# Rezero sum of two streams: three 64 KiB slots with the scaled operand multiplied in place, instead of two wide and two narrow buffers with a fused multiply-add

## The chip, the cores and the metric

The kernel runs on one core of a Trainium2 chip. The metric is device time in microseconds (us). The kernel before took 151.99 us, the median of three runs from 151.8 to 152.13. A profile is one execution recorded by the hardware profiler; its times count from the first instruction of the program.

## The reference

```python
B, S, D = 512, 32, 640
x     : (512, 32, 640) bf16
fx    : (512, 32, 640) bf16
alpha : (1,) bf16

def reference(x, fx, alpha):
    return x + alpha * fx
```

Each of x, fx and the result is 20.97 MB. Every element of x and fx is read once, every element of the result is written once, and there is one multiplication and one addition for each.

## The kernel before, in words

The three arrays are seen as 128 rows, one for each partition of the on-chip memory, of 81,920 elements (160 KiB) each. A unit K is 1,024 elements (2 KiB). The work is cut along the row, and differently for x and fx: x and the result in pieces of 32, 32 and 16 units (64, 64 and 32 KiB a partition), fx in pieces of 16, 16, 19, 16 and 13 units (32, 32, 38, 32 and 26 KiB). Two buffers of 64 KiB a partition hold pieces of x (`x_t`), two of 38 KiB hold pieces of fx (`f_t`). A third piece of x therefore needs the first buffer back, which is free once the first store has landed; a third piece of fx needs a VectorE pass to be over.

VectorE works on each overlap of a piece of fx with a piece of x, in one instruction, `scalar_tensor_tensor` (L92): it multiplies fx by alpha and adds x, and writes the sum over x. There are six of these. Alpha comes as a single value; a matrix product with a row of ones (L115) spreads it over the 128 partitions and VectorE copies it from PSUM to the fp32 tile `a_f` (L117).

Every transfer is issued by SyncE, whose queue works in program order: an issue that has to wait holds up all later ones. The order is written out by hand in `PLAN`, where `x i` and `f j` are loads (L77 and L85), `c j i` is a pass on VectorE, `s i` is a store (L104), and `a` fetches alpha (L111 and after). The first piece of x is cut into three transfers, of 8, 28 and 28 KiB a partition:

```python
X = [(0, 32), (32, 64), (64, 80)]
FX = [(0, 16), (16, 32), (32, 51), (51, 67), (67, 80)]
X_CUTS = {0: (4, 18)}
# order: x0  a  f0 f1 x1  c00  f2  c10  s0  f3 x2  c21  f4  c31 c32  s1  c42  s2
```

A load of 38 KiB a partition moves 4,864 KB in one transfer, spread over 16 DMA engines, eight partitions to each; a packet is the row of one partition.

At the end a no-op on SyncE waits for everything but the last store, which the exit itself waits for.

Of the kernel before, what the change touches and what calls it, by code (L numbers as in the profile page):

```python
# [2 lines left out]

# [4 lines left out]

ACT = mybir.ActivationFunctionType
ALU = mybir.AluOpType  # L10
F32 = mybir.dt.float32
BF16 = mybir.dt.bfloat16

K = 1024
P = 128


X = [(0, 32), (32, 64), (64, 80)]
FX = [(0, 16), (16, 32), (32, 51), (51, 67), (67, 80)]

X_CUTS = {0: (4, 18)}
PLAN = """
x 0
a
f 0
f 1
x 1
c 0 0
f 2
c 1 0  # L30
s 0
f 3
x 2
c 2 1
f 4
c 3 1
c 3 2
s 1
c 4 2
s 2  # L40
"""


@with_exitstack
def kernel(
    ctx: ExitStack,
    tc: tile.TileContext,
    x: bass.AP,
    fx: bass.AP,
    alpha: bass.AP,  # L50
    out: bass.AP,
):

    nc = tc.nc
    xv = x.flatten_outer_dims().rearrange("(p n) d -> p (n d)", p=P)
    fxv = fx.flatten_outer_dims().rearrange("(p n) d -> p (n d)", p=P)  # L60
    ov = out.flatten_outer_dims().rearrange("(p n) d -> p (n d)", p=P)
    assert xv.shape[1] == X[-1][1] * K == FX[-1][1] * K

    consts = ctx.enter_context(tc.tile_pool(name="consts", bufs=1))
    psum = ctx.enter_context(tc.tile_pool(name="psum", bufs=1, space=bass.MemoryType.PSUM))
    wide = ctx.enter_context(tc.tile_pool(name="wide", bufs=2))
    fs = ctx.enter_context(tc.tile_pool(name="fs", bufs=2))
    ctx.enter_context(tc.manual_schedule())

    xt, ft = {}, {}  # L70
    done = []

    def load_x(i):
        a, b = X[i]
        xt[i] = wide.tile([P, max(e - s for s, e in X) * K], x.dtype, tag="x", name="x_t")
        for c, d in pairwise((a, *X_CUTS.get(i, ()), b)):
            r = nc.sync.dma_start(  # L77
                out=xt[i][:, (c - a) * K : (d - a) * K], in_=xv[:, c * K : d * K]
            )
            done.append(r)  # L80

    def load_f(j):
        a, b = FX[j]
        ft[j] = fs.tile([P, max(e - s for s, e in FX) * K], fx.dtype, tag="f", name="f_t")
        r = nc.sync.dma_start(out=ft[j][:, : (b - a) * K], in_=fxv[:, a * K : b * K])  # L85
        done.append(r)

    def compute(j, i):
        (fa, fb), (xa, xb) = FX[j], X[i]
        a, b = max(fa, xa), min(fb, xb)  # L90
        piece = xt[i][:, (a - xa) * K : (b - xa) * K]
        r = nc.vector.scalar_tensor_tensor(  # L92
            out=piece,
            in0=ft[j][:, (a - fa) * K : (b - fa) * K],
            scalar=lanes["a_f"][:],
            in1=piece,
            op0=ALU.mult,
            op1=ALU.add,
        )
        done.append(r)  # L100

    def store(i):
        a, b = X[i]
        r = nc.sync.dma_start(out=ov[:, a * K : b * K], in_=xt[i][:, : (b - a) * K])  # L104
        done.append(r)

    lanes = {}

    def alpha_to_lanes():
        a_1 = consts.tile([1, 1], alpha.dtype, name="a_1")  # L110
        done.append(nc.sync.dma_start(out=a_1[:], in_=alpha[None, :]))  # L111
        ones = consts.tile([1, P], alpha.dtype, name="ones")
        nc.vector.memset(ones[:], 1.0)  # L113
        a_ps = psum.tile([P, 1], F32, name="a_ps")
        done.append(nc.tensor.matmul(a_ps[:], ones[:], a_1[:], start=True, stop=True))  # L115
        lanes["a_f"] = consts.tile([P, 1], F32, name="a_f")
        nc.vector.tensor_copy(out=lanes["a_f"][:], in_=a_ps[:])  # L117

    does = {"x": load_x, "f": load_f, "c": compute, "s": store, "a": alpha_to_lanes}
    for step in PLAN.split("\n"):  # L120
        if step:
            what, *of = step.split()
            does[what](*map(int, of))


    rest = nc.sync.nop(nofuse=True)
    info = mybir.DependencyInfo(mybir.DependencyClass.Sync, mybir.DependencyReason.DATA)
    for i in done[:-1]:
        tc.add_manual_dep(rest.ins, i.ins.name, info, reason="all but the last store")


# [1 line left out]
_INS = ['x', 'fx', 'alpha']  # L133
_OUTS = [((512, 32, 640), 'bfloat16')]


# [23 lines left out]
```

## Time and profile before

| | |
|---|---|
| median of three runs | 151.99 us (151.8 to 152.13) |
| profiled execution, first to last instruction | 150.6 us; its own time outside the span is not recorded |
| bytes read / written | 41.94 MB / 20.97 MB |
| mean rate over the span | 418 GB/s |
| share of the DMA engines' time, queue q1 | 97.9% |
| VectorE busy | 86.8 us (58%) |
| PE and POOL busy | 0.2 us each |
| large transfers issued by SyncE | 13, and the one of alpha |

A row of a group gives line, engine, operation, output and inputs, shape, count, busy time and the mean of one in ns, and then the idle time of the engine before it with what ended it. A row of the timeline gives start and duration in us. "SPq" is SyncE's queue: its rows are issues, whose duration is the time to hand the transfer over and not the time to move it. In a row of the windows the last two numbers are the share of the DMA engines' time and the rate in GB/s; packets are counted in the window in which they begin. "Landing" is the moment at which a transfer's semaphore is complete.

### The profile page before, as it was taken

The page shows a single profiled execution, that of the slowest core. Times are in us where ns is not written, and L with a number is a line of the kernel's source. Part 1 is how long each engine was busy: PE and PEld are TensorE (multiplying, and loading weights), DVE is VectorE, ACT ScalarE, POOL GpSimd, SP SyncE. Part 2 cuts the span into 40 slices and gives each one's busy share as a digit, 9 for nine tenths or more (in the row PEclk, how much of TensorE's full clock was granted, in tenths as well). Part 3 has the DMA queues.
Part 4 walks back from the last instruction along what each step waited for, and adds up shares of the span by engine and source line. Part 5 has one row for each costly group of instructions (what it writes and reads, how often), then busy time and mean ns, then how long its engine had stood idle before and what let it go on. Part 6 is the DMA issues. An engine that isn't in the chain of part 4 may idle for free.

```text
span 150.6 us, 81 instructions
## 1 busy us (share of the span) xinstructions
PE 0.2 (0%) x1; PEld 0.1 (0%) x1; DVE 86.8 (58%) x8; POOL 0.2 (0%) x4
## 2 busy tenths in 40 slices
PE   0000000000000000000000000000000000000000
PEld 0000000000000000000000000000000000000000
DVE  0000000049999999970299999105999999980000
POOL 0000000000000000000000000000000000000000
DMA  5998999999969696999796997999999969698993
GB/s 183 461 472 381 480 390 418 444 479 444 583 278 557 278 557 278 496 455 341 309 557 296 539 487 313 444 426 418 418 434 410 618 278 557 296 539 374 426 435 157
DMA packets 1874, 62.92 MB, mean 418 GB/s; under 512 B 210, under 2 KB 210, under 8 KB 210
## 3 DMA queue, kind: packets, MB, share of 16 engines
q1 hardware_dynamic: 1874, 62.92, 97.9%
HBM read 41.94 MB, written 20.97 MB: 418 GB/s over the span
## 4 chain that ended last, share of the span: by engine, by line
DMA 53%; DVE 34%; SPq 1%; issue 0%; DVEq 0%
DMA f_t<-in_fx_dram 53%; DVE x_t L92 34%; SPq L77 1%; SPq L111 0%; DVEq L92 0%
## 5 line engine op out<-in xcount | busy, mean ns | idle before, releaser
L92 DVE SCALAR_TENSOR_TENSOR x_t<-f_t,a_f,x_t 128x16384 bf16<-128x16384 bf16 (+3 forms) x6 | 86.5, 14438 | 25.8 <-DMA f_t<-in_fx_dram 25.8
L117 DVE COPY a_f<-a_ps 128x1 f32<-128x1 f32 x1 | 0.2, 159 | 21.6 <-PE a_ps L115 21.6
L113 DVE MEMSET ones<- 1x128 bf16 x1 | 0.2, 165 | 0.8 <-PEq L144 0.8
L115 PE MATMUL a_ps<-a,ones 1*128 1x1 bf16 x1 | 0.2, 158 | 22.4 <-DMA a<-in_alpha_dram 22.4
L144 POOL MEMSET const-bfloat16-1.0<- 128x1 bf16 x1 | 0.1, 102 | 0.0
L144 POOL MEMSET const-uint8-127<- 128x1 uint8 x1 | 0.1, 102 | 0.0
L115 PEld LDWEIGHTS <-ones 1*128 1x128 bf16 x1 | 0.1, 100 | 1.0 <-DVE ones L113 1.0
L144 POOL MEMSET const-float32-1.0<- 128x1 f32 x1 | 0.1, 99 | 0.0
L144 POOL MEMSET const-float32-0.0<- 128x1 f32 x1 | 0.1, 98 | 0.2 <-issue 0.2
## 6 DMA issues: line engine op xcount, KB each, us to landing
f_t<-in_fx_dram SPq DMA_DIRECT2D x3, 4096.0 KB, 36.1
x_t<-in_x_dram SPq DMA_DIRECT2D x2, 3584.0 KB, 16.8
f_t<-in_fx_dram SPq DMA_DIRECT2D x1, 4864.0 KB, 24.6
x_t<-in_x_dram SPq DMA_DIRECT2D x1, 4096.0 KB, 19.3
out_dram<-x_t SPq DMA_DIRECT2D x1, 4096.0 KB, 14.9
f_t<-in_fx_dram SPq DMA_DIRECT2D x1, 3328.0 KB
x_t<-in_x_dram SPq DMA_DIRECT2D x1, 1024.0 KB, 4.7
out_dram<-x_t SPq DMA_DIRECT2D x2, 24.9
```

What stands on the lines that cost most here:

```text
L77: r = nc.sync.dma_start(out=xt[i][:, (c - a) * K : (d - a) * K], in_=xv[:, c * K : d * K])
L92: r = nc.vector.scalar_tensor_tensor(out=piece, in0=ft[j][:, (a - fa) * K : (b - fa) * K], scalar=lanes["a_f"][:], in1=piece, op0=ALU.mult ...
L113: nc.vector.memset(ones[:], 1.0)
L115: done.append(nc.tensor.matmul(a_ps[:], ones[:], a_1[:], start=True, stop=True))
L117: nc.vector.tensor_copy(out=lanes["a_f"][:], in_=a_ps[:])
L144: nc = _bacc.Bacc("TRN2", target_bir_lowering=False, num_devices=1)
```

## The change

Both inputs are now cut alike, in pieces of 64, 64 and 32 KiB a partition (a unit K is now 512 elements, 1 KiB). There are three slots of 64 KiB a partition, a, b and c. The first piece of fx goes to slot a, in transfers of 8 and 56 KiB; alpha follows; the first piece of x goes to b, the second of fx to c. VectorE multiplies a piece of fx by alpha in place (`tensor_scalar`), and adds it into the piece of x (`tensor_tensor`), six instructions in all. The second piece of x goes over the first piece of fx, in slot a, once that was added; the third pieces of fx and x share slot b, once the first store has landed. The order on SyncE is: fx0 (two transfers), alpha, x0, fx1, store 0, x1, fx2, x2, store 1, store 2. VectorE's is: multiply fx0, add x0, multiply fx1, add x1, multiply fx2, add x2. Fetching and spreading alpha is as before, as is the no-op at the end.

```diff
-K = 1024
+K = 512
...
-X = [(0, 32), (32, 64), (64, 80)]
-FX = [(0, 16), (16, 32), (32, 51), (51, 67), (67, 80)]
-
-X_CUTS = {0: (4, 18)}
...
+WIDE = 64
+PIECES = [(0, 64), (64, 128), (128, 160)]
+HEAD = 8
...
-    wide = ctx.enter_context(tc.tile_pool(name="wide", bufs=2))
-    fs = ctx.enter_context(tc.tile_pool(name="fs", bufs=2))
+    slots = ctx.enter_context(tc.tile_pool(name="slots", bufs=1))
...
+    slot = [slots.tile([P, WIDE * K], x.dtype, name=f"slot_{n}") for n in "abc"]
...
+    def move(out, in_):
+        r = nc.sync.dma_start(out=out, in_=in_)
+        done.append(r)
+        return r
...
+    def load(of, piece, at, cut=0):
...
+        a, b = piece
+        n, where = at
+        t = slot[n][:, where * K : (where + b - a) * K]
+        if cut:
+            move(t[:, : cut * K], of[:, a * K : (a + cut) * K])
+        move(t[:, cut * K :], of[:, (a + cut) * K : b * K])
+        return t
...
-        r = nc.vector.scalar_tensor_tensor(
-            out=piece,
-            in0=ft[j][:, (a - fa) * K : (b - fa) * K],
-            scalar=lanes["a_f"][:],
-            in1=piece,
-            op0=ALU.mult,
-            op1=ALU.add,
-        )
...
+    def scaled(f):
+        done.append(nc.vector.tensor_scalar(out=f, in0=f, scalar1=a_f[:], scalar2=None, op0=ALU.mult))
...
+    def added(xt, f):
+        done.append(nc.vector.tensor_tensor(out=xt, in0=xt, in1=f, op=ALU.add))
...
+    def store(piece, t):
+        a, b = piece
+        move(ov[:, a * K : b * K], t)
...
+    p0, p1, p2 = PIECES
+    f0 = load(fxv, p0, (0, 0), cut=HEAD)
...
+    x0 = load(xv, p0, (1, 0))
+    scaled(f0)
+    f1 = load(fxv, p1, (2, 0))
+    added(x0, f0)
+    scaled(f1)
+    store(p0, x0)
+    x1 = load(xv, p1, (0, 0))
+    added(x1, f1)
+    f2 = load(fxv, p2, (1, 0))
+    x2 = load(xv, p2, (1, WIDE // 2))
+    scaled(f2)
+    store(p1, x1)
+    added(x2, f2)
+    store(p2, x2)
```

More of the change, by code (lines that the diff above doesn't have):

```diff
@@ L1 @@
 from contextlib import ExitStack
-from itertools import pairwise
 import concourse.bass as bass
@@ L7 @@
 from concourse._compat import with_exitstack
-ACT = mybir.ActivationFunctionType
 ALU = mybir.AluOpType
 F32 = mybir.dt.float32
-BF16 = mybir.dt.bfloat16
-K = 1024
+K = 512
 P = 128
-X = [(0, 32), (32, 64), (64, 80)]
-FX = [(0, 16), (16, 32), (32, 51), (51, 67), (67, 80)]
-X_CUTS = {0: (4, 18)}
[L22 to L41, printed above, removed]
+WIDE = 64
+PIECES = [(0, 64), (64, 128), (128, 160)]
+HEAD = 8
 @with_exitstack
@@ L61 @@
     ov = out.flatten_outer_dims().rearrange("(p n) d -> p (n d)", p=P)
-    assert xv.shape[1] == X[-1][1] * K == FX[-1][1] * K
+    assert xv.shape[1] == PIECES[-1][1] * K
     consts = ctx.enter_context(tc.tile_pool(name="consts", bufs=1))
     psum = ctx.enter_context(tc.tile_pool(name="psum", bufs=1, space=bass.MemoryType.PSUM))
-    wide = ctx.enter_context(tc.tile_pool(name="wide", bufs=2))
-    fs = ctx.enter_context(tc.tile_pool(name="fs", bufs=2))
+    slots = ctx.enter_context(tc.tile_pool(name="slots", bufs=1))
@@ L68 @@
     ctx.enter_context(tc.manual_schedule())
-    xt, ft = {}, {}
+    slot = [slots.tile([P, WIDE * K], x.dtype, name=f"slot_{n}") for n in "abc"]
     done = []
[L73 to L78, printed above, removed]
-            )
-            done.append(r)
@@ L82, in load_f @@
[L82 to L85, printed above, removed]
-        done.append(r)
[L88 to L92, printed above, removed]
-            out=piece,
-            in0=ft[j][:, (a - fa) * K : (b - fa) * K],
-            scalar=lanes["a_f"][:],
-            in1=piece,
-            op0=ALU.mult,
-            op1=ALU.add,
-        )
-        done.append(r)
@@ L102, in store @@
[L102 to L123, printed above, removed]
+    def move(out, in_):
+        r = nc.sync.dma_start(out=out, in_=in_)
+        done.append(r)
+        return r
[7 more added lines that the diff above has]
+        return t
@@ new lines, in scaled @@
+    def scaled(f):
[7 more added lines that the diff above has]
+    f0 = load(fxv, p0, (0, 0), cut=HEAD)
+    a_1 = consts.tile([1, 1], alpha.dtype, name="a_1")
+    move(a_1[:], alpha[None, :])
+    ones = consts.tile([1, P], alpha.dtype, name="ones")
@@ new lines @@
+    nc.vector.memset(ones[:], 1.0)
+    a_ps = psum.tile([P, 1], F32, name="a_ps")
+    done.append(nc.tensor.matmul(a_ps[:], ones[:], a_1[:], start=True, stop=True))
+    a_f = consts.tile([P, 1], F32, name="a_f")
+    nc.vector.tensor_copy(out=a_f[:], in_=a_ps[:])
+    x0 = load(xv, p0, (1, 0))
[8 more added lines that the diff above has]
+    x2 = load(xv, p2, (1, WIDE // 2))
```

## The prediction

> **What bounds the kernel now.** I read the page first, then busy time by windows cut where a transfer begins, then the timeline of SyncE's queue, then groups by form. The page says how little is left to gain:
>
> ```profile
> span 150.6 us, 81 instructions
> ...
> PE 0.2 (0%) x1; PEld 0.1 (0%) x1; DVE 86.8 (58%) x8; POOL 0.2 (0%) x4
> ...
> q1 hardware_dynamic: 1874, 62.92, 97.9%
> HBM read 41.94 MB, written 20.97 MB: 418 GB/s over the span
> ```
>
> All transfers go through one queue, and its packets fill 97.9% of the 16 engines' time. The chain of waits names f_t loads and VectorE, but VectorE waits for transfers that never stop: the bound is the stream of 62.92 MB, and only holes in it are worth money. The windows show where they are (time, length, busy time of PE, PEld, DVE, POOL, clock, DMA share, GB/s):
>
> ```profile
> 0.00:1.73 1.73, 0.00 (x0) 0.10 (x1) 0.17 (x1) 0.20 (x4) 1.00 0.00 0
> 1.73:4.57 2.84, 0.00 (x0) 0.00 (x0) 0.00 (x0) 0.00 (x0) 1.00 1.00 363
> ...
> 21.53:40.99 19.46, 0.16 (x1) 0.00 (x0) 8.90 (x2) 0.00 (x0) 1.00 1.00 431
> 40.99:60.32 19.33, 0.00 (x0) 0.00 (x0) 19.33 (x2) 0.00 (x0) 1.00 1.00 434
> 60.32:68.94 8.62, 0.00 (x0) 0.00 (x0) 6.41 (x1) 0.00 (x0) 1.00 1.01 433
> 68.94:73.14 4.20, 0.00 (x0) 0.00 (x0) 0.00 (x0) 0.00 (x0) 1.00 1.01 296
> 73.14:92.46 19.32, 0.00 (x0) 0.00 (x0) 18.21 (x1) 0.00 (x0) 1.00 1.00 434
> 92.46:119.70 27.24, 0.00 (x0) 0.00 (x0) 18.69 (x3) 0.00 (x0) 1.00 1.00 433
> 119.70:139.02 19.32, 0.00 (x0) 0.00 (x0) 15.09 (x2) 0.00 (x0) 1.00 1.00 434
> ```
>
> Nothing moves until 1.73; the first MB comes at 363 GB/s, 2.84 us where 434 would need 2.42, so a pipe that starts empty loses 0.42. After that loads and stores alike run at 431 to 434, but for one stretch just ahead of the first store: 4.20 us at 296 move 1.24 MB, which 433 would move in 2.87. I call it the slow stretch; it costs 1.3 us and nothing in the profile names its cause.
>
> ```profile
> 0.73 1.33 SPq L77 DMA_DIRECT2D x_t<-in_x_dram  x3
> ...
> 49.56 0.33 SPq L85 DMA_DIRECT2D f_t<-in_fx_dram  x1
> 66.76 0.35 SPq L104 DMA_DIRECT2D out_dram<-x_t  x1
> 67.16 0.49 SPq L85 DMA_DIRECT2D f_t<-in_fx_dram  x1
> ...
> 117.40 17.96 SPq L104 DMA_DIRECT2D out_dram<-x_t  x2
> ```
>
> Every issue after the first comes well ahead of its turn: the first store is issued at 66.76 and moves from 73.14, the second at 117.40 and moves from 119.70. That lead keeps the queue full. The only start on an empty queue is 0.73 to 1.73: 1.00 us from issue to first packet. The price of a VectorE pass:
>
> ```profile
> L92 DVE SCALAR_TENSOR_TENSOR x_t<-f_t,a_f,x_t 128x16384 bf16<-128x16384 bf16 x2 | 34.5, 17282 | 9.5 <-DMA f_t<-in_fx_dram 9.5
> L92 DVE SCALAR_TENSOR_TENSOR x_t<-f_t,a_f,x_t 128x13312 bf16<-128x13312 bf16 x2 | 28.2, 14085 | 8.8 <-DMA f_t<-in_fx_dram 8.8
> ```
>
> The difference, 3.197 us for 3,072 elements, is 1.04 ns each, and 0.2 us are fixed. A fused pass over 32,768 elements would take 2 x 17.07 + 0.2 = 34.3 us.
>
> **The change part by part.** *The bytes* are the same, so the stream at full rate is too. *Longer rows, fewer transfers:* the packets of an engine fall from 104 to 80 (eight a transfer: thirteen large transfers become ten). Two loads in 32 KiB rows took 19.46 us, one in 64 KiB rows 19.33: 0.13 for eight packets, though part of it may be noise, as 90 KiB in rows of 32, 32 and 26 KiB took 27.24 against 27.18 at the price of 64 KiB rows. For 24 packets that bounds the gain between 0.1 and 0.4; I take 0.2, nearer to the longer and cleaner row.
>
> *The start:* the first issue is 8 KiB a partition as before, so 1.73 and the ramp stay. Alpha stood behind 64 KiB of x and now stands behind 64 KiB of fx; it is in the lanes at 22.7 as before (PE waited 22.4 us for it). The five transfers to f1 need no wait. 128 KiB a partition have moved at 41.0, and the one that ends there (second f_t load before, x0 after) lands at about 41.9: issued at 2.9, the largest f_t landing is 39.0 us. 192 KiB have moved at 60.3.
>
> *VectorE:* each fused pass becomes a multiply and an add. No row prices either. From above, each takes a fused pass's 1.04 ns an element, 34.3 us; from below, only the fixed 0.2 us. I take half the fused price each, an estimate: the fused pass does both operations, and if its price is theirs added, the two halves together cost what it did: 17.2 + 0.1, so 17.3 us on 32,768 elements, and 8.7 on 16,384. The multiplies have room at that price: f0's runs from 22.7 to 40.0, below x0's landing at 41.9 (it may take 19.2); f1's lies under store and load of the next 39 us; f2's ends at 126.
>
> The Trainium skill, VectorE: DVE Perf Modes, section "The perf-mode tier table (the rule you actually need)", says that bf16 adds of two tensors in SBUF run at twice, and one-tensor multiplies at four times, the basic rate. Beside the row's 1.04 ns that makes 17.1 and 8.5 us before fixed cost, as estimates by that page; no row here shows either form. By the unhalved row the time would be the 214 us of rival three; by the page it is my forecast.
>
> *First hand-over:* the add of x0 runs from 41.9 to 59.2. Behind it on SP wait the store p0 and, behind that, the load x1, which needs the same add (it overwrites f0's slot). SP issues 0.03 us after VectorE ends (66.73 to 66.76), so at 59.25; the first packet is ready 1.00 later, at 60.25, and f1's packets end at 60.32. The lead of 2.3 to 6.4 us before shrinks to the bare 1.0. From below it costs nothing; from above the empty pipe's 0.42 and the whole 1.0, together 1.4. I take 0.3, nearer to 0.42 as both ends coincide within 0.1.
>
> The Trainium skill, DMA: Bandwidth & Descriptors, section "Latency and other measured facts", gives about 0.6 us to a first byte; the trace differs, with 1.00. By that page the store would be ready at 59.85, both hand-overs would cost nothing, and the time would be 151.8.
>
> *Middle:* store p0 moves until 79.9, x1 until 99.3. SP stands at f2, whose half of slot b needs store p0 landed (0.5 after its end, 80.5); x2, store p1 and p2 queue behind it. That wait is covered: x1 has 19 us left. f2 ends at 108.9, x2 at 118.6. *Second hand-over:* x1 lands at 100.2, its add ends at 117.5, the store is issued at 117.55 and ready at 118.55, against x2's end at 118.6: again 0.3. *End:* multiply f2 to 126.2, add x2 to 134.9, its store issued 3 us before store p1 ends at 138.2. The tail is as before: 32 KiB rows, landing, exit.
>
> *Slow stretch:* kept, 1.3 us, at zero change; bounds 0 and -1.3.
>
> Sum: 150.6 + 0.3 + 0.3 - 0.2 = span 151.0. What lies around the profiled span is shown only through the runs (151.8 to 152.13), whose median is 1.4 above it; so 152.4.
>
> **The rivals.** *One, faster: the slow stretch goes.* If it comes with a store that queues early behind a load (6.4 us ahead at 66.76), the late stores don't have it. For it: at 117.40 a store came 2.3 ahead and the load in front stayed at 433. Against: one instance; it may belong to the first store wherever it stands, or to a disturbance that the other runs lack. 152.4 - 1.3 = 151.1; 150.5 with both hand-overs free.
>
> *Two: the hand-overs cost 1.1 us more each.* The add decides: from 17.3 us for 32,768 elements upward, each us counts twice. At 1.4 each the time is 152.4 + 2.2 = 154.6. For it: the margin of 0.1. Against: an engine's last packets spread over half a us, so not all wait.
>
> *Three: a pass with one operation is no cheaper an element.* f0's multiply ends at 57.1, x0's add at 91.4, store p0 moves 92.5 to 111.9, x1 lands at 131.7, its add ends at 166.1, multiply f2 183.3, add x2 200.6, last store 201.6 to 211.3: a span of 212.4, 214 us. Against: six passes that all carry two operations say nothing of a pass with one. The Trainium skill's page VectorE: DVE Perf Modes, in the section named above, has it otherwise.
>
> *The change does little:* 64 KiB rows carry x's second load and two stores already, and no engine but the queue binds, so with free hand-overs it is 151.8; that lies in the forecast's own range.
>
> **How the numbers follow.** Forecast 0.48 (151.7 to 153.0); one 0.32; two 0.12; three 0.05; others 0.03. About 0.2% (0.3 us: 151.69 to 152.29) is what a measurement can tell from no change. Faster: nearly all of one and a little of the forecast's lower end, 0.32. Same: a third of the forecast and a rest, 0.19. Slower: the rest of the forecast, two and three, 0.49. The range leaves out three, the others, and the ends of one and two: 150.6 to 154.0.
>
> **What would show it.** Right: GB/s within 1% of 434 but for short dips at 60 and 118; store issues near 59 and 117.5; adds of 17.3 us. Rival one: no stretch below 400 between 5 and 147. Two: a window of zero ahead of a store. Three: passes of 34 us. Wrong beyond all: loads in 64 KiB rows below 430, or VectorE slowing under the stream.

## The result, and the profile after

The changed kernel took 152.37 us, the median of ten runs from 152.12 to 153.08; the kernel before took 152.00 us in its ten runs beside them (151.80 to 152.14). The ratio is 1.003, with a 95% interval from 1.0018 to 1.0042: slower by 0.37 us. The span is recorded for every run of the experiments below, and time less span is 1.8 us for both kernels. So the span of 150.6 us that the prediction started from was 0.4 above what the kernel before usually shows (150.2, the median of 151.97 less 1.8), and the changed kernel's median span is 150.6.

The page of the changed kernel has the lines that answer to those of before:

```profile
span 150.6 us, 74 instructions
...
PE 0.2 (0%) x1; PEld 0.1 (0%) x1; DVE 65.4 (43%) x8; POOL 0.2 (0%) x4
...
q1 hardware_dynamic: 1442, 62.92, 97.6%
...
L64 DVE TENSOR_TENSOR slot_a<-slot_a,slot_c 128x32768 bf16<-128x32768 bf16 x1 | 17.2, 17224 | 31.8 <-DMA slot_a<-in_x_dram 31.8
...
L61 DVE TENSOR_SCALAR slot_a<-slot_a,a_f 128x32768 bf16<-128x32768 bf16 x1 | 8.8, 8754 | 0.0
```

VectorE's time fell by 21.4 us and nothing came of it, because the queue is as full as it was. An add of 32,768 elements takes 17.2 us, a multiply 8.75. The windows of the changed kernel, cut where packets of a transfer begin (time, length, busy time of PE, PEld, DVE and POOL, clock, DMA share, GB/s):

```profile
40.94:60.30 19.36, 0.00 (x0) 0.00 (x0) 17.22 (x1) 0.00 (x0) 1.00 1.00 433
60.30:77.21 16.91, 0.00 (x0) 0.00 (x0) 8.75 (x1) 0.00 (x0) 1.00 1.00 434
77.21:85.07 7.86, 0.00 (x0) 0.00 (x0) 0.00 (x0) 0.00 (x0) 1.00 1.04 400
77.62:86.63 9.01, 0.00 (x0) 0.00 (x0) 0.00 (x0) 0.00 (x0) 1.00 0.84 349
85.07:99.56 14.49, 0.00 (x0) 0.00 (x0) 0.00 (x0) 0.00 (x0) 1.00 1.00 434
99.56:119.62 20.06, 0.00 (x0) 0.00 (x0) 18.08 (x2) 0.00 (x0) 1.00 0.97 418
119.62:139.04 19.42, 0.00 (x0) 0.00 (x0) 12.23 (x2) 0.00 (x0) 1.00 1.00 432
```

The first hand-over, at 60.3, shows no hole: 433 ahead of it, 434 behind. The stretch below 434 just ahead of the first store is gone as well, and a new one lies at 77 to 87, at the change from the first store to the load of x1. The third and fourth rows show the same 48 packets, three of each engine (3.15 MB, 7.25 us at 434), twice: the third row on the engine that is first, from the start of its first such packet to the start of the one behind them, and the fourth the same on the engine that is last. The first engine loses 0.6 us there and the last 1.8: the 16 engines fall apart. At the second hand-over the early engines do wait (418), but what counts is the last engine, and for it two rows of VectorE's timeline are better, because here a load has landed only after its last engine was done (the packets of f1 end between 60.31 and 60.53, and the pass that waits for them starts at 60.95):

```profile
58.91 0.35 SPq L46 DMA_DIRECT2D out_dram<-slot_b  x1
...
60.95 8.75 DVE L61 TENSOR_SCALAR slot_c<-slot_c,a_f 128x32768 bf16<-128x32768 bf16 x1 [2.08 <-DMA slot_c<-in_fx_dram]
81.23 0.33 SPq L46 DMA_DIRECT2D slot_b<-in_fx_dram  x1
...
101.54 17.22 DVE L64 TENSOR_TENSOR slot_a<-slot_a,slot_c 128x32768 bf16<-128x32768 bf16 x1 [31.83 <-DMA slot_a<-in_x_dram]
...
118.79 0.34 SPq L46 DMA_DIRECT2D out_dram<-slot_a  x1
```

VectorE starts at 60.95 and 101.54 because f1 and x1 have landed. Between them a store and a load of 64 KiB a partition went by, 38.7 us at full rate; it took 40.6, so the last engine lost 1.9. Behind that, the second store landed 21.4 us after its issue, at 140.2: from 101.5 that is 38.7 us for another 128 KiB. The last engine lost nothing at the second hand-over.

Counted in the same way for the kernel before, from the landing of its second load of x (issue 3.40, 57.8 us, so 61.2) to that of its first store (issue 66.76, 26.9 us, so 93.66), 102 KiB a partition took 32.46 us where the full rate gives 30.83: 1.6 lost in its slow stretch. The load that waits for that store is issued at that moment:

```profile
93.66 0.33 SPq L77 DMA_DIRECT2D x_t<-in_x_dram  x1
```

### The profile page after: what moved, and what is told of

Its sections match the earlier page's. It is cut to its first block, busy times and chain, and to the rows that moved or that the text cites. A ratio compares the mean times of both kernels' runs of the same rounds, so it can differ in the third digit from the quotient of the medians.

```text
span 150.6 us, 74 instructions
## 1 busy us (share of the span) xinstructions
PE 0.2 (0%) x1; PEld 0.1 (0%) x1; DVE 65.4 (43%) x8; POOL 0.2 (0%) x4
## 4 chain that ended last, share of the span: by engine, by line
DMA 54%; DVE 27%; issue 5%; SPq 1%; DVEq 0%
DMA slot_a<-in_x_dram 28%; DMA slot_b<-in_x_dram 26%; DVE slot_b L64 17%; DVE slot_a L64 6%; DVE slot_b L61 3%; SPq L46 1%; DVEq L64 0%
## 5 line engine op out<-in xcount | busy, mean ns | idle before, releaser
L64 DVE TENSOR_TENSOR slot_a<-slot_a,slot_c 128x32768 bf16<-128x32768 bf16 x1 | 17.2, 17224 | 31.8 <-DMA slot_a<-in_x_dram 31.8
L64 DVE TENSOR_TENSOR slot_b<-slot_b,slot_a 128x32768 bf16<-128x32768 bf16 x1 | 17.2, 17224 | 10.2 <-DMA slot_b<-in_x_dram 10.2
L61 DVE TENSOR_SCALAR slot_c<-slot_c,a_f 128x32768 bf16<-128x32768 bf16 x1 | 8.8, 8754 | 2.1 <-DMA slot_c<-in_fx_dram 2.1
L61 DVE TENSOR_SCALAR slot_a<-slot_a,a_f 128x32768 bf16<-128x32768 bf16 x1 | 8.8, 8754 | 0.0
L64 DVE TENSOR_TENSOR slot_b<-slot_b 128x16384 bf16<-128x16384 bf16 x1 | 8.7, 8693 | 0.0
L61 DVE TENSOR_SCALAR slot_b<-slot_b,a_f 128x16384 bf16<-128x16384 bf16 x1 | 4.5, 4479 | 0.0
```

The lines of the kernel that those rows point to most:

```text
L61: done.append(nc.vector.tensor_scalar(out=f, in0=f, scalar1=a_f[:], scalar2=None, op0=ALU.mult))
L64: done.append(nc.vector.tensor_tensor(out=xt, in0=xt, in1=f, op=ALU.add))
```

## The experiments

Kernels of one set ran on the same chip and share their runs of the kernel before: its medians were 151.97 (first set), 151.85 (second) and 151.92 us (third). Theory one was the prediction: late hand-overs make the difference and both kernels keep the slow stretch.

### Both kernels again

No edit; what repeats?

> The kernel before, unchanged, to see what repeats. Theory one (the kernels differ by late hand-overs and both keep the slow stretch): the span is 150.6 again within 0.3 us, and a stretch near 300 GB/s that costs about 1.3 us lies at 69 to 73 us again, just ahead of the first store. Rival (the slow stretch is a disturbance from outside): it lies elsewhere or is missing, and where it is missing the span is 149.3. Rival on the time outside the span: time less span is 1.4 here against 1.8 for the changed kernel, so that the 0.37 us lie outside the span.

> The changed kernel, unchanged. Theory one: 152.4 us, the slow stretch again at 77 to 84 us, at the change from the first store to the second load of x, and store 1 beginning about 0.5 us late on the engines that are done first. Rival (disturbance): the stretch moves or goes.

The kernel before took 151.98 us and the changed one 152.47 (ratio 1.0034, interval 1.0022 to 1.0045). The slow stretches repeat in place. Windows of the kernel before, and then of the changed kernel from its first and from its last engine:

```profile
60.34:68.97 8.63, 0.00 (x0) 0.00 (x0) 6.47 (x1) 0.00 (x0) 1.00 1.00 433
68.97:72.96 3.99, 0.00 (x0) 0.00 (x0) 0.00 (x0) 0.00 (x0) 1.00 1.01 312
72.96:92.27 19.31, 0.00 (x0) 0.00 (x0) 18.37 (x1) 0.00 (x0) 1.00 1.00 434
```

```profile
77.20:82.76 5.56, 0.00 (x0) 0.00 (x0) 0.00 (x0) 0.00 (x0) 1.00 1.03 377
77.59:84.05 6.46, 0.00 (x0) 0.00 (x0) 0.00 (x0) 0.00 (x0) 1.00 0.80 325
```

So in both traces of each kernel the stretch lies where that kernel's order of work puts it, which speaks against a disturbance from outside. In this pair it cost the kernel before 1.1 us (3.99 against 2.87) and the changed kernel 0.7 on the first engine and 1.6 on the last (against 4.83 for its 32 packets). The changed kernel's VectorE timeline gives about the same, 40.35 us from f1's landing to x1's and so 1.7 lost:

```profile
61.01 8.75 DVE L61 TENSOR_SCALAR slot_c<-slot_c,a_f 128x32768 bf16<-128x32768 bf16 x1 [2.06 <-DMA slot_c<-in_fx_dram]
101.36 17.22 DVE L64 TENSOR_TENSOR slot_a<-slot_a,slot_c 128x32768 bf16<-128x32768 bf16 x1 [31.60 <-DMA slot_a<-in_x_dram]
```

Time less span was 1.8 for both, which ends the rival that the difference lies outside the span.

### Large adds and stores in halves

```diff
-    added(x0, f0)
+    H = WIDE // 2 * K
+    added(x0[:, :H], f0[:, :H])
+    added(x0[:, H:], f0[:, H:])
...
-    store(p0, x0)
+    store((0, 32), x0[:, :H])
+    store((32, 64), x0[:, H:])
```

and the same for x1 and its store.

> Both large adds and both large stores cut in halves, so that a store of 32 KiB a partition is issued 8 us before its turn. Theory one (the late hand-overs cost the difference): 151.8 to 152.0 us, 0.4 to 0.6 below the changed kernel, less about 0.1 for 16 more packets an engine. Rival (the hand-overs cost nothing, as no engine that ends last waits in the profile): 152.4 to 152.5.

152.20 us, 0.27 below the changed kernel of the same set and between the two expectations (ratio to before 1.0013, 1.0001 to 1.0025). Its profiled execution took 152.49 us, one of its slowest and no less than the changed kernel, so the trace can't say where the 0.27 came from. It does show what became of the stretch. Windows of this kernel:

```profile
40.82:57.74 16.92, 0.00 (x0) 0.00 (x0) 15.85 (x2) 0.00 (x0) 1.00 1.00 434
57.74:61.33 3.59, 0.00 (x0) 0.00 (x0) 1.44 (x1) 0.00 (x0) 1.00 1.03 292
61.33:80.69 19.36, 0.00 (x0) 0.00 (x0) 8.75 (x1) 0.00 (x0) 1.00 1.00 433
80.69:117.05 36.36, 0.00 (x0) 0.00 (x0) 15.88 (x2) 0.00 (x0) 1.00 1.00 433
117.05:119.76 2.71, 0.00 (x0) 0.00 (x0) 2.71 (x2) 0.00 (x0) 1.00 1.05 387
```

With the first store queued at 50.6, well ahead, the slow stretch is back in front of it, as in the kernel before (3.59 us for 2.42), and the change at 80.7 is clean. In front of the second store there is a smaller one (2.71 for 2.42). So an early store does not only take a late hand-over away: the stretch comes back in front of it.

### Adds that end 2.3 us later

```diff
+    def late(t):
+        part = t[:, : 16 * K]
+        done.append(nc.vector.tensor_scalar(out=part, in0=part, scalar1=1.0, scalar2=None, op0=ALU.mult))
...
+    late(x0)
     added(x0, f0)
...
+    late(x1)
     added(x1, f1)
```

> Ahead of each of the two large adds VectorE multiplies a quarter of x by 1.0 in place (8,192 elements, about 2.3 us by the rows 8,754 ns for 32,768 and 4,479 ns for 16,384 elements). Theory one (an add that ends later is paid in full, and twice): the first store has 0.4 us to spare by the profile, the second none, so 2.3 - 0.4 + 2.3 = 4.2 us more than the changed kernel, 156.6 us. Rival (the hand-overs have slack that the issue rows do not show, 1 us each or more): at most 2.6 us more, 155.0.

155.14 us: 2.7 more than the changed kernel for 4.7 us of lateness (two extra passes of 2.29 us and their gaps). That is just above the rival's bound of 2.6, and far from theory one's 4.2. SyncE's timeline, with a window of the first hole behind it:

```profile
61.47 0.35 SPq L46 DMA_DIRECT2D out_dram<-slot_b  x1
...
122.19 0.34 SPq L46 DMA_DIRECT2D out_dram<-slot_a  x1
```

```profile
60.80:62.30 1.50, 0.00 (x0) 0.00 (x0) 1.50 (x2) 0.00 (x0) 1.00 0.00 0
62.30:79.28 16.98, 0.00 (x0) 0.00 (x0) 7.81 (x1) 0.00 (x0) 1.00 1.00 432
79.28:84.87 5.59, 0.00 (x0) 0.00 (x0) 0.00 (x0) 0.00 (x0) 1.00 1.03 375
```

The store issued at 61.47 has its first packet at 62.3: 0.84 us, less than the 1.00 that the prediction took from the program's start. Between the last engine's last packet, which ends at 60.78, and the first of the store's packets nothing moves for 1.5 us, while the extra pass had put the add off by 2.33. So the unchanged hand-over had some 0.8 us to spare on the last engine, and lateness first eats that up.

### The turn back to loads made just in time

Theory two: a transfer of the other direction that is queued long ahead of its turn brings the stretch.

```diff
-    store(p0, x0)
+    first = move(ov[:, : 58 * K], x0[:, : 58 * K])
+    move(ov[:, 58 * K : 64 * K], x0[:, 58 * K :])
     x1 = load(xv, p1, (0, 0))
+    tc.add_manual_dep(done[-1].ins, first.ins.name, info, reason="x1 late")
```

> The first store is cut into 58 and 6 KiB a partition, and the load of x1 waits until the first of them has landed, so that it is issued about 1.3 us ahead of its turn and not 20. Theory two (the slow stretch is paid where a transfer of the other direction has been queued well ahead of its turn): the stretch at 77 to 84 us goes and no other comes, 1.0 us less, 151.4 us. Theory one (the stretch is a fixed price of the first change from stores to loads or the like): it stays and the time is 152.4 to 152.6. Third (the late issue of x1 leaves a hole as large): 152.4 with a hole near 80 us in place of the stretch.

152.54 us (ratio 1.0051, 1.0038 to 1.0064). The load of x1 was issued at 78.89 and its packets begin between 79.9 and 80.7, yet the stretch stays, now in its first packets. Timeline, then windows:

```profile
78.89 0.34 SPq L47 DMA_DIRECT2D slot_a<-in_x_dram  x1
```

```profile
60.38:77.98 17.60, 0.00 (x0) 0.00 (x0) 8.75 (x1) 0.00 (x0) 1.00 1.00 432
79.94:83.09 3.15, 0.00 (x0) 0.00 (x0) 0.00 (x0) 0.00 (x0) 1.00 0.90 297
```

The window at 297 GB/s holds almost all first packets of that load, which take about 3.15 us where 64 KiB at full rate take 2.42. Theory two falls in this form: a short lead doesn't avoid it.

### The first store of the kernel before made late

```diff
+FX_CUTS = {2: (48,)}
...
+        if i == 0:
+            tc.add_manual_dep(r.ins, first[2].ins.name, info, reason="store late")
```

(`first[2]` is the first part of the third load of fx, which `FX_CUTS` cuts.)

> In the kernel before, the third load of fx is cut into 32 and 6 KiB a partition, and the first store waits until the first of them has landed: it is issued at about 70.5 us, 1.4 us ahead of its turn at 71.9, and not 5. Theory two: the slow stretch moves from 69 to 73 us to the next turn, from this store to the load behind it at 91 us, as in the changed kernel; 152.0 to 152.4 us. Theory one: it stays at 69 to 73 us, 152.0.

152.99 us (ratio 1.0078, 1.0061 to 1.0095), more than any theory had. The stretch did move, as theory two said: the store was issued at 71.20, and the windows are

```profile
60.49:71.90 11.41, 0.00 (x0) 0.00 (x0) 6.44 (x1) 0.00 (x0) 1.00 1.00 427
...
89.04:93.37 4.33, 0.00 (x0) 0.00 (x0) 4.33 (x1) 0.00 (x0) 1.00 1.04 363
```

with no slow stretch ahead of the store and one at its end, where the next load follows. So a late first store alone moves the stretch from the front of that store to its end, as the change did, without any of the change's other parts. It does not account for the 1.1 us that this kernel lost. In this trace three of the 16 engines also fell back by 0.6 to 0.8 us near 118, in the last packets of the last load of fx, just ahead of the second store, and stayed behind to the end; the trace doesn't say why.

### A small transfer near the start

Theory three: the stretch is paid once, at the first change of direction, and a small one may pay it cheaply.

```diff
+    small = consts.tile([P, K], x.dtype, name="small")
+    nc.vector.memset(small[:], 0.0)
...
+    early = move(ov[:, 159 * K : 160 * K], small[:])
```

placed between the two parts of the first load.

> A small store (1 KiB a partition of zeros, to the end of the result, which the last store writes over later) is queued behind the first 1 MB load. Its bytes are 131 KB, 0.3 us. If the slow stretch is a price paid once, at the first turn of direction with both sides queued: it comes near 5 us or goes into the start, and the stretch at 77 to 84 us goes; 151.5 to 152.7 us. If every turn that is queued ahead at large transfers can pay: the stretch at 77 to 84 us stays and the time is 152.7 us.

151.83 us: ratio to before 1.0003 (0.9994 to 1.0011), where the changed kernel had 1.0034 in the first set (152.47 us). The control has a load in place of that store:

> Control for the early store in the changed kernel: in its place a load of the same 1 KiB a partition, into the same small tile, which nothing reads. Theory three: a load is no turn, the stretch at 77 to 84 us stays at 1.0 us and the 0.35 us at the start come on top, 152.7 us. Rival (any small transfer near the start sets the engines apart and so shortens the stretch): 151.8 us, as with the store.

151.74 us: ratio to before 0.9984 (0.9976 to 0.9993), so it is the one kernel of the study that is faster than both, by 0.16% over the kernel before. VectorE's timeline of the kernel with the store, and then of the one with the load:

```profile
61.80 8.75 DVE L62 TENSOR_SCALAR slot_c<-slot_c,a_f 128x32768 bf16<-128x32768 bf16 x1 [2.06 <-DMA slot_c<-in_fx_dram]
100.95 17.23 DVE L65 TENSOR_TENSOR slot_a<-slot_a,slot_c 128x32768 bf16<-128x32768 bf16 x1 [30.40 <-DMA slot_a<-in_x_dram]
```

```profile
61.67 8.75 DVE L62 TENSOR_SCALAR slot_c<-slot_c,a_f 128x32768 bf16<-128x32768 bf16 x1 [2.04 <-DMA slot_c<-in_fx_dram]
100.86 17.23 DVE L65 TENSOR_TENSOR slot_a<-slot_a,slot_c 128x32768 bf16<-128x32768 bf16 x1 [30.43 <-DMA slot_a<-in_x_dram]
```

f1 lands 0.7 to 0.9 us later than in the changed kernel, which is the small transfer's price at the start; but from f1's landing to x1's it is 39.2 us in both, 0.5 above the full rate, where the changed kernel took 40.6 and, in its second trace, 40.4. The gain is in the stretch, of which the last engine keeps 0.5 us and no longer 1.7 to 1.9. The engine that is first still loses about what it lost in the changed kernel, 0.4 and 0.65 us against 4.83 for 32 packets (windows with the store, then with the load), so what shrank is the distance between the engines:

```profile
77.81:83.04 5.23, 0.00 (x0) 0.00 (x0) 0.00 (x0) 0.00 (x0) 1.00 1.01 401
```

```profile
77.58:83.06 5.48, 0.00 (x0) 0.00 (x0) 0.00 (x0) 0.00 (x0) 1.00 1.00 383
```

And the gain comes with a load as with a store, so theory three falls: the direction of the small transfer doesn't matter.

The kernel before was given the same small store:

```diff
+            if i == 0 and c == 0:
+                early.append(nc.sync.dma_start(out=ov[:, 80 * K - 512 : 80 * K], in_=small[:]))
```

> The kernel before with the same small early store (1 KiB a partition of zeros behind the first 1 MB load, written over by the last store). Theory three (the slow stretch is a price that the first store and the first turn bring once, and that a small early store takes over in part): the stretch at 69 to 73 us shrinks from 1.3 to about 0.5 us, the start loses 0.35, so 0.5 less than the kernel before: 151.4 us, faster than both kernels. Rival (the early store helped the changed kernel alone, through its late hand-overs): the stretch stays and 0.35 us come on top, 152.2 us.

152.05 us (ratio 1.001, 1.0001 to 1.0019). Neither expectation: the last transfer ahead of the first store lost 0.4 us an engine, and not 1.2 as in the second trace of the kernel before, but the price at the start (its second load of x lands at 62.0 and not at 61.2 or 61.3) was about as large as the gain.

The last of these kernels is the changed one with the small early store and the halves together:

> The changed kernel with the small early store and with both large adds and stores in halves. Theory (late hand-overs and the slow stretch are separate costs, 0.27 and 0.6 us by the kernels that took one of them away): 152.4 - 0.27 - 0.6 = 151.5 us, faster than both kernels. Rival (the halves only trade a late hand-over for a dip at a store that queues early): 151.8 us.

152.32 us (ratio 1.0035, 1.0018 to 1.0053): the two gains do not add up, they are lost. The profiled execution was the slowest of its twelve (153.3 us), so its trace is no picture of the median. In it one engine alone fell 0.6 us behind all others near 62 and as much again near 120, both times in the last packets of a load just ahead of a store, and set the end.

### One part of the change alone: two passes in the kernel before

```diff
-        r = nc.vector.scalar_tensor_tensor(
...
+        f = ft[j][:, (a - fa) * K : (b - fa) * K]
+        done.append(nc.vector.tensor_scalar(out=f, in0=f, scalar1=lanes["a_f"][:], scalar2=None, op0=ALU.mult))
+        r = nc.vector.tensor_tensor(out=piece, in0=piece, in1=f, op=ALU.add)
```

> One part of the change alone: the kernel before with multiply in place and add in place of each fused pass. By 8,754 and 17,224 ns for 32,768 elements two passes take 26.0 us where the fused took 34.4, so VectorE is busy about 65 us. Theory (VectorE is covered by the stream): no change, 151.9 us within 0.2, with the slow stretch again ahead of the first store. Rival (the earlier stores move the stretch or shorten it): 0.3 us or more to either side.

151.96 us (ratio 0.9999, 0.9991 to 1.0008): no difference, with VectorE busy for 66.4 us and not 86.8, and the first store issued at 58.85 and not 66.76. The stretch stays ahead of that store (windows):

```profile
60.48:70.56 10.08, 0.00 (x0) 0.00 (x0) 0.00 (x0) 0.00 (x0) 1.00 1.00 432
70.56:72.68 2.12, 0.00 (x0) 0.00 (x0) 0.00 (x0) 0.00 (x0) 1.00 1.01 294
```

It is shorter here, 0.7 us over the full rate for its 16 packets (2.12 against 1.44) and not 1.1 to 1.3, yet the median is no lower (the profiled execution took 151.79). So this trace gives no support to the reading that a shorter stretch alone makes a kernel faster.

### One part left out: the fused pass in the changed kernel

```diff
-        done.append(nc.vector.tensor_tensor(out=xt, in0=xt, in1=f, op=ALU.add))
+        done.append(
+            nc.vector.scalar_tensor_tensor(
+                out=xt, in0=f, scalar=a_f[:], in1=xt, op0=ALU.mult, op1=ALU.add
+            )
+        )
...
-    scaled(f0)
...
-    scaled(f1)
...
-    scaled(f2)
```

> The changed kernel's slots and order with the fused multiply-add of before in place of multiply and add: one pass of 34.4 us on 32,768 elements where the add takes 17.2. Theory one: the first store is issued at 76 and begins at 77 us, 16.6 us late, the second at 150.5 and begins at 151.4, and the time is 183 us: each us of the add beyond 17.3 is paid twice. Rival (the schedule bears longer passes): below 170 us.

185.06 us in its one run. The group row of the fused pass, and the two holes:

```profile
L65 DVE SCALAR_TENSOR_TENSOR slot_b<-slot_a,a_f,slot_b 128x32768 bf16<-128x32768 bf16 x1 | 34.4, 34352 | 19.4 <-DMA slot_b<-in_x_dram 19.4
```

```profile
60.90:77.28 16.38, 0.00 (x0) 0.00 (x0) 15.52 (x1) 0.00 (x0) 1.00 0.00 0
137.00:152.90 15.90, 0.00 (x0) 0.00 (x0) 15.90 (x2) 0.00 (x0) 1.00 0.00 0
```

The pass is 17.1 us longer than the add, twice, and the kernel 32.6 us longer than the changed one in the first set: all but 1.7 us of it is paid. The new slots and order need the cheap add; the order of before doesn't.

## Why the prediction was right, and where it was not

The number was right, 152.4 for 152.37, and so was the sign, but the number in part by luck. The main reason held: the queue is the bound, its bytes and its rate do not change, and 21.4 us less on VectorE are worth nothing, as the two passes in the kernel before show by themselves. The terms of the sum did worse than the sum. With each term as it was measured below, the sum is 150.2 for the span before, 0 for the hand-overs, 0.3 for the stretch, -0.2 for the rows and 1.8 around the span, together 152.1; the remaining 0.3 us has no place in it. Of the signs that the prediction had named, the adds took their 17.2 us and the first store was issued at 58.91, but there was no dip at 60, the one at 118 (418 GB/s) came on the early engines alone, the second store was issued at 118.79 and not 117.5, and the stretch at 77 to 87 was not among them.

*VectorE's price.* The add was taken at 17.3 us and took 17.2. The multiply was taken at 17.3 and took 8.75, a quarter of the fused price an element; as worked out, that changes nothing, since up to 19.2 us it was hidden. The Trainium skill, VectorE: DVE Perf Modes, section "The perf-mode tier table (the rule you actually need)", had both: twice and four times the basic rate, 17.1 and 8.5 us before fixed cost, and these traces agree. Rival three is out.

*The hand-overs, 0.3 us each: wrong.* At the first, 433 and 434 GB/s on both sides of 60.3 leave no room for a hole. At the second the early engines wait, but from x1's landing to the second store's landing the last engine runs at the full rate. The term was 0 and 0 on the path. Three things were off. The time from issue to first packet is 0.84 us and not 1.00. At the first hand-over the add ended earlier than forecast, so that the store was issued at 58.91 and not 59.25 and, with the 0.84, was ready at 59.75, ahead of the first engine's end at 60.31. At the second the forecast had one end for 16 engines, where the last is 1.5 us behind the first and hides the store's arrival. The 2.7 us paid for 4.7 us of lateness fit this. The Trainium skill, DMA: Bandwidth & Descriptors, section "Latency and other measured facts", has about 0.6 us to the first byte; the measured 0.84 lies between it and the row that was used. What the prediction worked out from that page, free hand-overs, was right.

*The slow stretch, kept at zero change: kept, but neither in its place nor quite in its size.* It moved from the first store's front to its end. Between landings, so on the last engine, it cost the kernel before 1.6 and, in the repetition, 1.4 us (61.3 to 93.5), and the changed kernel 1.9 and 1.7. That is 0.3 more on average, in a term that the prediction had at 0. The prediction's own timeline has no place for the stretch either: from 60.3 to x1's end at 99.3 and store p1's at 138.2 it runs at the full rate, while its sum keeps the 1.3 us, so the second store was forecast at 117.55 and came 1.2 us later. Rival one, that it goes with a late store, was half right: it left the place that was named, and came back at the next turn. The first store of the kernel before, made late, does the same.

*Longer rows, -0.2 us.* No run took this by itself, but the packets of the traces bear its size out: with the median times of each length, among them 1.213 us for 32 KiB and 2.418 for 64 KiB, an engine's 104 packets before add up to 145.4 or 145.5 us and its 80 packets now to 145.3, which is 0.1 to 0.2 less.

*What lies around the span* was set at 1.4 us from a profile that was 0.4 above its median. It is 1.8, and the predicted span of 151.0 was 0.4 too high for the same reason. The two errors cancel, which is luck.

The traces do not explain all of the 0.37 us. The two profiled executions of the kernel before ended at 150.6 and 150.3 and the two of the changed kernel at 150.6 and 150.4, which is closer together than the medians, and fits a stretch that is 0.3 larger against the 0.2 that the rows save. The other 0.3 us of the medians is in neither pair. Shown is that the hand-overs cost the last engine nothing, that the stretch moved and spreads the engines further apart, and that the changed kernel loses its whole disadvantage when the stretch shrinks on the last engine (151.83 and 151.74 us). That the stretch is the cause of the 0.37 is the likeliest reading of these, but no run changes it alone, and the kernel before with two passes had a shorter stretch and the same time.

What the stretch itself is stays open. It lay in the same place in the second trace of either kernel; a first store queued 5 to 14 us ahead has it in front, a first store that comes at the last moment has it behind; a load issued just in time has it too; a small transfer some 70 us earlier, in either direction, makes it smaller by half or more on the last engine. No theory tried here predicts all four.

## What to carry to other kernels

When a single queue is busy for 97% of the span, count what each edit does to its holes, and count them on the engine that ends last, between landings: here the early engines waited 0.7 us at the second hand-over and the last one lost nothing. A faster pass on a covered engine buys freedom of order and no time; if the new order spends that freedom on a later store, nearly every further us of the pass is paid at each hand-over, as the fused pass in the new slots shows. And a change of 0.2% needs the spans of many runs beside the profile, since one profile can be off by as much as the effect.

## What the runs showed of the hardware that was not expected

Loads and stores move at the same 432 to 434 GB/s, but one of the first changes between them cost 0.4 to 1.9 us, by kernel and engine, and in both traces of the kernel before and of the changed one it lay in the same place: one or two packets an engine at 292 to 312 GB/s where it was worst. In the changed kernel it set the 16 engines 1.5 us apart, and they stayed so for some 19 us, until a hole let the early ones wait; half of it stayed to the end. An added transfer of 131 KB at 5 us, a load that nobody reads, made the kernel about 0.7 us faster although it cost 0.7 us itself. In two further traces one engine or three fell back by 0.6 to 0.8 us more than the others, each time in the last packets of a load just ahead of a store.
